# Gathered rows of experts 1 to 7 turned by VectorE instead of TensorE

## The chip, the cores and the metric

The kernel runs on one core of one Trainium2 chip. The time is device microseconds of one execution. Before the change it is 1012.99 us in the median of 3 runs (1011.71 to 1014.88).

## The reference

Three stages follow each other on 4 x 576 = 2304 tokens of 512 features, all in fp32. First an attention of 8 heads that goes through 32 packed keys a head. Then a noisy top-2 routing to 8 experts, of which each computes `relu(x @ w1[e]) @ w2[e]` (512 to 1024 to 512) on its tokens. Then one dense layer of 512 to 2048 to 512 with a sigmoid gate.

```python
p_packed = sm_attn(p, k, v)                 # softmax attention, 32 rows a head
x = sm_attn(q, p_packed, p_packed)          # to (2304, 512): row = token, columns = head, then dimension
noisy_logits = x @ w_gate + np.log1p(np.exp(x @ w_noise)) * noise
top2 = np.argpartition(-noisy_logits, 2, axis=1)[:, :2]     # softmax weights over the two
for e in range(8):
    for k in range(2):
        mask = top2[:, k] == e
        out[mask] += top2_w[mask, k, None] * (np.maximum(x[mask] @ w1[e], 0.0) @ w2[e])
h = out @ w_in
return (h / (1.0 + np.exp(-h))) @ w_out
```

## The kernel before

Every fp32 operand of a large product is kept as a high and a low part, and a product is three matmuls (high by high, high by low, low by high).

The attention stage makes the rows of `x` in tiles of 128 tokens: two matmuls a tile (L419) give 256 features each, ScalarE copies them into the tile `xr` (L424), and SyncE stores it to `xs` in DRAM (L426). Beside it run the routing (`route`) and the load of expert 0's weights: `load` (L124) fetches a piece of 512 KB into one of three buffers `raw` by one DMA on SyncE, and `split` (L109) makes the high part on ScalarE (L111) and the low part on VectorE, for expert 0 on GpSimd (L112). The routing ends with `idx` (L513), the token of every slot: 8 experts x 5 tiles x 128 slots.

The experts' stage goes through experts 0 to 7, each in a short block of two tiles (256 tokens) and a long block of three (384). A block has eight steps. A step makes 128 hidden features of the block (`first`, 12 matmuls, L167 to L169, into one of two PSUM buffers `hps`), ScalarE evicts them as `hh` (L190), VectorE subtracts for `hl` (L191), and two steps later `second` (L177 to L179) adds their part to the block's output.

The tokens of a block come from `xs`: `fetch` (L150) lets GpSimd issue one indirect DMA a tile (L155), which gathers 128 rows of 2 KB into one of five buffers `xg`. `transposed` (L141) then turns the tile, since the product wants features on partitions: four TensorE transposes of 128x128 into PSUM (L145), a copy to the high part `xha` or `xhb` on ScalarE (L147), and a subtraction to the low part `xla` or `xlb` on VectorE (L148). The hooks between the steps (`hook_a`, `hook_b`) place the turn of the other block's next tiles, the loads and splits of the next expert's weights, and the conversion of pieces of the last layer's weights (`load64`, L638 to L642, through two scratch buffers `t64`, stored to DRAM at L669). Expert 0's two tiles are gathered and turned ahead of its first block, its three others in the last steps of that block, and expert 1's first two behind it.

The order on each engine is set by a planner that places each instruction by a simulated timeline; in the experts' stage some are pinned to program order (`pin`), among them the splits and the TensorE transposes. Each engine works through its own order. SyncE issues all plain DMAs in one order, GpSimd the indirect ones.

Of the kernel before, what the change touches and what calls it, by code (L numbers as in the profile page):

```python
# [7 lines left out]
F32 = mybir.dt.float32  # L8
# [11 lines left out]
P = 128  # L20
# [3 lines left out]
ET = 5  # L24
# [20 lines left out]
def body(ctx: ExitStack, tc: tile.TileContext, q, k, v, p, wg, wn, noise, w1, w2, w_in, w_out, out):  # L45
# [32 lines left out]
    V.tensor_scalar(sbase, iota8, float(CAP), ident[:, 0:1], op0=OP.mult, op1=OP.mult)  # L78
    ilo = const.tile([P, P], F32)
    G.iota(ilo, pattern=[[1, P]], base=0, channel_multiplier=0, allow_small_or_imprecise_dtypes=True)  # L80
# [15 lines left out]
    idx = const.tile([P, E * ET], I32)  # L96
    idx0 = const.tile([P, TA], I32)
    few = const.tile([P, E], F32)

    M = {"pin": False, "w": 384, "hb": 3}  # L100

    def pin(ins):
        if M["pin"]:
            tc.keep_in_program_order(ins)
# [18 lines left out]

    def load(dst, src, c, eng=V):  # L124

        hi, lo = dst
        raw = raws.tile([P, 1024], F32, name="raw", tag="raw")
        nc.sync.dma_start(raw.rearrange("p (c f) -> p c f", c=c), src.rearrange("(c p) f -> p c f", p=P))
        later.append(lambda: split(hi, lo, raw, eng))

    def load_w1(dst, e, i, eng=V):
        load(dst[i], w1[e, :, i * 256:(i + 1) * 256], 4, eng)

# [7 lines left out]
    def transposed(src, xh, xl, j):  # L141

        ps = M["t"].tile([P, 4, P], F32, name="tps", tag="tr")
        for c in range(4):
            pin(T.transpose(ps[:, c, :], src[:, c * P:(c + 1) * P], ident))  # L145
        s = slice(j * P, (j + 1) * P)
        A.activation(xh[:, :, s], ps, AF.Copy)  # L147
        V.tensor_tensor(xl[:, :, s], ps, xh[:, :, s].bitcast(F32), op=OP.subtract)  # L148

    def fetch(src, ix, c0, n):  # L150
# [66 lines left out]
    with ExitStack() as ax:  # L217
# [150 lines left out]
        def unpacked(t, n, lg):  # L368
# [45 lines left out]
            for i in range(n):  # L414
                xr = sb.tile([P, 2, 256], F32, name="xr")
# [10 lines left out]
                nc.sync.dma_start(xs[r0:r0 + P, :], xr.rearrange("p a b -> p (a b)"))  # L426
            yield

        def route(t0, n, lg):
# [178 lines left out]
        for j, xg in enumerate(fetch(xs[0:EARLY * P, :], idx0, 0, TA)):  # L608
            transposed(xg, *X["a"], j)
        cnt = const.tile([P, E], F32)  # L610
        most = const.tile([P, 1], I32)
        rows = []
        for f in expert_block(0, 0, TA, X["a"]):
            run(r1, 2)
            if f == 4:
                for _ in r1:
                    pass
                rows = fetch(xs[:, :], idx, TA, TB) + fetch(xs[:, :], idx, ET, TA)
                c = pMx.tile([P, E], F32, name="c", tag="m")
                T.matmul(c, ones, seen_b, start=True, stop=True)  # L620
                V.tensor_tensor(cnt, c, few, op=OP.max)
                V.tensor_reduce(most, cnt, axis=AX.X, op=OP.max)
            if f > 4:
                transposed(rows[f - 5], *X["b"], f - 5)
        flush(0)
        for j in range(TA):
            transposed(rows[TB + j], *X["a"], j)

# [17 lines left out]
    def routed():  # L646
        ctx = mx = ExitStack()
        with mx:
# [29 lines left out]
            def combine(m):  # L678
# [4 lines left out]
                for j in range(n):  # L683
# [8 lines left out]
                    V.scalar_tensor_tensor(y[0], y[1], gates[:, t, 1:2], y[0], op0=OP.mult, op1=OP.add)  # L692
                    transposed(y[0], xh, xl, j)

# [42 lines left out]
            def hook_a(e, f):  # L737
                tick()
                if box["b"] and f:
                    transposed(box["b"].pop(0), *X["b"], TB - 1 - len(box["b"]))  # L740
                if f % 2:
# [6 lines left out]
                if f == 5 and e < E - 1:  # L748
                    box["a"] = fetch(xs[:, :], idx, (e + 1) * ET, TA)

            def hook_b(e, f):
# [17 lines left out]
                if f == 5:  # L769
                    box["b"] = fetch(xs[:, :], idx, (e + 1) * ET + TA, TB)  # L770

# [29 lines left out]
def general(tc, xs, ident, iota8, chosen, gates, w1, w2, w_in, w_out, out, load64):  # L801
# [3 lines left out]
    with tc.tile_pool(name="gc", bufs=1) as gc:  # L805
# [9 lines left out]
        with tc.For_i(0, NT, 1) as t, ExitStack() as fx:  # L815
# [21 lines left out]
            nc.sync.dma_start(x, xs[bass.ds(t * P, P), :])  # L837
            xT = turned(x, "xT")
            x2 = fs.tile([P, DM], F32, name="x2")
# [61 lines left out]
```

## Time and profile before

| | |
|---|---|
| median of 3 runs | 1012.99 us |
| the profiled execution's own time | 1011.33 us |
| its span, first to last instruction | 1009.4 us |
| TensorE busy | 974.0 us (96%) |
| VectorE busy | 436.5 us (43%) |
| ScalarE busy | 348.2 us (34%) |
| GpSimd busy | 208.4 us (21%) |
| mean granted TensorE clock | 0.981 |

The attention stage fills the time up to about 124 us, the experts' stage that up to about 600 us, the last layer the rest. PE is TensorE, DVE VectorE, ACT ScalarE, POOL GpSimd and SP SyncE; a q behind the name is the engine's queue of DMA issues and waits. A busy share is a mean over stages with different limits; the stage itself says what bounds it.

### The profile page before, as it was taken

The page shows a single profiled execution, that of the slowest core. Times are in us where ns is not written, and L with a number is a line of the kernel's source. Part 1 is how long each engine was busy: PE and PEld are TensorE (multiplying, and loading weights), DVE is VectorE, ACT ScalarE, POOL GpSimd, SP SyncE. Part 2 cuts the span into 40 slices and gives each one's busy share as a digit, 9 for nine tenths or more (in the row PEclk, how much of TensorE's full clock was granted, in tenths as well). Part 3 has the DMA queues.
Part 4 walks back from the last instruction along what each step waited for, and adds up shares of the span by engine and source line. Part 5 has one row for each costly group of instructions (what it writes and reads, how often), then busy time and mean ns, then how long its engine had stood idle before and what let it go on. Part 6 is the DMA issues. An engine that isn't in the chain of part 4 may idle for free.

```text
span 1009.4 us, 14342 instructions
## 1 busy us (share of the span) xinstructions
PE 974.0 (96%) x5672; PEld 836.8 (83%) x5672; DVE 436.5 (43%) x845; ACT 348.2 (34%) x631; POOL 208.4 (21%) x221
## 2 busy tenths in 40 slices
PE   6998899999999999999999998999999999999996
PEld 4775688999999989999999997888888888888885
DVE  4556763665657566565534457312212221111111
ACT  3575323433434343343423354322222222222221
POOL 2162011100101010010100117433323322222221
PEclk9988699999999999999999999999999999999999
DMA  9993223576757566574623346201111010001001
GB/s 254 254 281 121 90 74 115 188 219 185 229 151 235 176 201 214 186 230 149 227 84 115 125 160 185 74 21 32 32 42 42 21 48 6 1 0 42 1 1 44
DMA packets 80472, 122.47 MB, mean 121 GB/s; under 512 B 14608, under 2 KB 47376, under 8 KB 80400
## 3 DMA queue, kind: packets, MB, share of 16 engines
q1 hardware_dynamic: 74320, 101.57, 32.1%
q0 software_dynamic: 6080, 19.93, 6.6%
q8 instruction: 46, 0.75, 0.3%
q14 instruction: 26, 0.21, 0.1%
HBM read 93.17 MB, written 28.31 MB: 120 GB/s over the span
## 4 chain that ended last, share of the span: by engine, by line
PE 91%; DMA 3%; SPq 2%; DVE 1%; ACT 1%; POOL 1%; issue 1%; ACTq 0%; DVEq 0%; POOLq 0%
PE hps L167 14%; PE hps L168 14%; PE hps L169 14%; PE acc L177 14%; PE acc L178 14%; PE acc L179 13%; PE tps L145 2%; PE xp L419 2%; PE s L388 1%; DMA vm<-in_v_dram 1%; DMA km<-in_k_dram 1%; PE qp L381 1%; DMA y<-ys,slots 1%; SPq L236 0%; PE s L321 0%
## 5 line engine op out<-in xcount | busy, mean ns | idle before, releaser
L702 POOL TENSOR_TENSOR gl<-sg,gh 128x512 fp32r<-128x512 f32 (+1 forms) x80 | 96.0, 1201 | 253.9 <-ACT gh L701 238.6
L190 ACT ACTIVATE hh<-hps 128x384 fp32r<-128x384 f32 (+1 forms) x128 | 56.1, 438 | 253.7 <-PE hps L169 244.3
L698 DVE TENSOR_TENSOR sg<-hps,sg 128x512 f32<-128x512 f32 (+1 forms) x80 | 50.7, 635 | 195.8 <-ACT sg L697 195.4
L191 DVE SCALAR_TENSOR_TENSOR hl<-hps,hh 128x384 fp32r<-128x384 f32 (+1 forms) x128 | 62.8, 490 | 141.8 <-ACT hh L190 137.1
L155 POOL DMA_INDIRECT xg<-xs,idx x40 | 42.8, 1069 | 348.4 <-PE tps L145 296.7
L697 ACT ACTIVATE sg<-hps 128x512 f32<-128x512 f32 (+1 forms) x80 | 44.3, 553 | 187.9 <-PE hps L169 186.6
L701 ACT ACTIVATE gh<-sg 128x512 fp32r<-128x512 f32 (+1 forms) x80 | 47.1, 589 | 79.8 <-DVE sg L698 74.9
L688 POOL DMA_INDIRECT y<-ys,slots x36 | 37.5, 1043 | 117.1 <-DMA ys<-ysb 78.8
L148 DVE TENSOR_TENSOR xla<-tps,xha 128x512 fp32r<-128x512 f32 x26 | 18.0, 691 | 30.0 <-ACT xha L147 30.0
L419 PE MATMUL xp<-ppBD,a2T 128*128 128x272 f32 (+1 forms) x80 | 27.1, 481 | 2.1 <-ACT xr L51 1.7
L148 DVE TENSOR_TENSOR xlb<-tps,xhb 128x512 fp32r<-128x512 f32 x32 | 22.0, 687 | 15.1 <-ACT xhb L147 13.8
L691 DVE TENSOR_SCALAR y<-y,gates 128x512 f32<-128x512 f32 x18 | 10.3, 570 | 39.2 <-DMA y<-ys,slots 39.2
L692 DVE SCALAR_TENSOR_TENSOR y<-y,gates,y 128x512 f32<-128x512 f32 x18 | 14.7, 817 | 26.1 <-DMA y<-ys,slots 26.1
L147 ACT ACTIVATE xhb<-tps 128x512 fp32r<-128x512 f32 x32 | 19.1, 596 | 19.2 <-PE tps L145 18.7
L145 PEld LDWEIGHTS tps<-ident,xg 128*128 128x128 f32 x160 | 19.9, 141 | 5.3 <-issue 0.4
L145 PE MATMUL tps<-ident,xg 128*128 128x128 f32 x160 | 23.9, 272 | 0.2 <-issue 0.2
L641 DVE SCALAR_TENSOR_TENSOR t<-raw,t 128x512 int32<-128x512 int32 x32 | 22.2, 693 | 1.1
L642 DVE SCALAR_TENSOR_TENSOR t<-raw,t 128x512 int32<-128x512 int32 x32 | 22.1, 690 | 0.9
L147 ACT ACTIVATE xha<-tps 128x512 fp32r<-128x512 f32 x26 | 15.5, 597 | 19.7 <-PE tps L145 19.7
L638 ACT ACTIVATE t<-raw 128x512 f32<-128x512 f32 x32 | 21.1, 659 | 0.0
L388 PE MATMUL s<-ppT,qT 128*128 128x64 f32 x128 | 20.2, 315 | 0.0
L167 PE MATMUL hps<-xha,wa3h 128*128 128x256 f32 (+1 forms) x56 | 17.7, 316 | 2.2 <-DVE wb3l L112 1.5
(439 smaller groups left out, 2954.2 us busy)
## 6 DMA issues: line engine op xcount, KB each, us to landing
raw<-in_moe_w_dram SPq DMA_DIRECT2D x64, 512.0 KB
ys<-ysb SPq DMA_DIRECT2D x40, 256.0 KB
raw<-in_moe_w_in_dram SPq DMA_DIRECT2D x16, 512.0 KB
raw<-in_moe_w_out_dram SPq DMA_DIRECT2D x16, 512.0 KB
xs<-xr SPq DMA_DIRECT2D x18, 256.0 KB
km<-in_k_dram SPq DMA_DIRECT2D x8, 512.0 KB
vm<-in_v_dram SPq DMA_DIRECT2D x8, 512.0 KB
qm<-in_q_dram SPq DMA_DIRECT2D x8, 512.0 KB
```

The source lines that it names most:

```text
L145: pin(T.transpose(ps[:, c, :], src[:, c * P:(c + 1) * P], ident))
L167: T.matmul(ps, wh[:, c, s], xh[:, c, :n], start=c == 0, stop=False)
L168: T.matmul(ps, wh[:, c, s], xl[:, c, :n], start=False, stop=False)
L169: T.matmul(ps, wl[:, c, s], xh[:, c, :n], start=False, stop=c == 3)
L177: T.matmul(y, hh[:, s], wh[:, f % 2, :], start=f == 0, stop=False)
L178: T.matmul(y, hh[:, s], wl[:, f % 2, :], start=False, stop=False)
L179: T.matmul(y, hl[:, s], wh[:, f % 2, :], start=False, stop=f == last)
L190: A.activation(hh, ps, AF.Relu)
L191: V.scalar_tensor_tensor(hl, ps, 0.0, hh.bitcast(F32), op0=OP.max, op1=OP.subtract)
L419: T.matmul(xp[sl], aT[:, 2 * i + g, sl], ppBD[b, g], start=True, stop=True)
L698: V.tensor_tensor(sg, ps, sg, op=OP.mult)
L702: G.tensor_tensor(gl, sg, gh.bitcast(F32), op=OP.subtract)
```

## The change

The rows in `xs` are stored in another feature order. Feature number 128 b + 32 a + j (b and a from 0 to 3, j from 0 to 31) now stands in column 128 a + 32 b + j. ScalarE's copy into `xr` writes that order.

For experts 1 to 7 a tile is now fetched by four indirect DMAs instead of one. Each gathers a quarter of a row (512 bytes) for 128 partitions. In quarter g, the partitions 32 a to 32 a + 31 take quarter a of the rows of tokens 32 g to 32 g + 31. Their index `idx4` is made once behind `idx`: 16 small TensorE matmuls repeat the 32 indices in each group of partitions, and VectorE multiplies by 4 and adds a. VectorE then turns the whole 128x512 tile in blocks of 32x32 by one instruction into a scratch tile of the two `t64` buffers. ScalarE copies it to the high part and VectorE subtracts for the low part, both from SBUF.

Expert 0 keeps the gather of whole rows and the turn on TensorE. Its features then come out in the stored order, and so its `w1` pieces are loaded in that order, by four DMAs of 32 partitions instead of one. The path for overfull experts at the end of the program, which these inputs don't take, reorders the features it reads.

```diff
-    ilo = const.tile([P, P], F32)
+    ilo = dif
...
+    idx4 = const.tile([P, 4, E * ET], I32)
+    quad = const.tile([P, 1], F32)
+    for a in range(4):
+        V.memset(quad[32 * a:32 * a + 32], float(a))
...
-        nc.sync.dma_start(raw.rearrange("p (c f) -> p c f", c=c), src.rearrange("(c p) f -> p c f", p=P))
+        if runs:
+            for b in range(4):
+                nc.sync.dma_start(raw[32 * b:32 * b + 32].rearrange("j (a f) -> j a f", a=4),
+                                  src[b * P:(b + 1) * P].rearrange("(a j) f -> j a f", a=4))
+        else:
+            nc.sync.dma_start(raw.rearrange("p (c f) -> p c f", c=c), src.rearrange("(c p) f -> p c f", p=P))
...
-        load(dst[i], w1[e, :, i * 256:(i + 1) * 256], 4, eng)
+        load(dst[i], w1[e, :, i * 256:(i + 1) * 256], 4, eng, e == 0)
...
+    def runs(t):
+        return t.rearrange("p (a b j) -> p b a j", a=4, b=4)
+
+    def fetch4(c0, n):
+        tiles = []
+        for c in range(c0, c0 + n):
+            xg = M["s"].tile([P, DM], F32, name="xg", tag="xg", bufs=5)
+            for g in range(4):
+                G.indirect_dma_start(out=xg[:, g * P:(g + 1) * P], out_offset=None,
+                                     in_=xs[:, :].rearrange("n (a f) -> (n a) f", a=4),
+                                     in_offset=bass.IndirectOffsetOnAxis(ap=idx4[:, g, c:c + 1], axis=0))
+            tiles.append(xg)
+        return tiles
+
+    def turned4(src, xh, xl, j):
+        xt = M["s"].tile([P, 512], F32, name="xturn", tag="t64")
+        V.transpose(xt, src)
+        v = xt.rearrange("p (g b i) -> p b g i", g=4, b=4)
+        hi, lo = (x[:, :, j * P:(j + 1) * P].rearrange("p b (g i) -> p b g i", g=4) for x in (xh, xl))
+        pin(A.activation(hi, v, AF.Copy))
+        V.tensor_tensor(lo, v, hi.bitcast(F32), op=OP.subtract)
...
-                    cp(A, xr[:, g, :], xp[:, 0:256])
+                    cp(A, runs(xr)[:, 2 * g:2 * g + 2], xp[:, 0:256].rearrange("p (b a j) -> p b a j", b=2, a=4))
...
+                V.tensor_scalar(idx_f, idx_f, 0.0, float(N - 1), op0=OP.max, op1=OP.min)
+                i4 = pMx.tile([P, 4, E * ET], F32, name="i4", tag="m")
+                for g in range(4):
+                    for a in range(4):
+                        T.matmul(i4[32 * a:32 * a + 32, g, :], ident[:, 32 * g:32 * g + 32], idx_f, start=True, stop=True,
+                                 tile_position=(0, 32 * a))
+                V.tensor_scalar(idx4, i4, 4.0, quad[:, 0:1], op0=OP.mult, op1=OP.add)
...
-                rows = fetch(xs[:, :], idx, TA, TB) + fetch(xs[:, :], idx, ET, TA)
+                rows = fetch(xs[:, :], idx, TA, TB)
+                ahead = fetch4(ET, TA)
...
-            transposed(rows[TB + j], *X["a"], j)
+            turned4(ahead[j], *X["a"], j)
...
-                    transposed(box["b"].pop(0), *X["b"], TB - 1 - len(box["b"]))
+                    turned4(box["b"].pop(0), *X["b"], TB - 1 - len(box["b"]))
...
-                    box["a"] = fetch(xs[:, :], idx, (e + 1) * ET, TA)
+                    box["a"] = fetch4((e + 1) * ET, TA)
...
-                    transposed(box["a"].pop(0), *X["a"], TA - 1 - len(box["a"]))
+                    turned4(box["a"].pop(0), *X["a"], TA - 1 - len(box["a"]))
...
-                    box["b"] = fetch(xs[:, :], idx, (e + 1) * ET + TA, TB)
+                    box["b"] = fetch4((e + 1) * ET + TA, TB)
```

SyncE's order where expert 0's first weight pieces (`raw`) are loaded, among the last loads of q, k and v; first before, then after.

```order
L128 DMA raw<-in_moe_w_dram 128x4x256 x3
L247 DMA qm<-in_q_dram 128x4x256
L238 DMA vr<-in_v_dram 64x4x64
L238 DMA kr<-in_k_dram 64x4x64
L247 DMA qm<-in_q_dram 128x4x256
L238 DMA vr<-in_v_dram 64x4x64
L247 DMA qm<-in_q_dram 128x4x256 x2
L128 DMA raw<-in_moe_w_dram 128x4x256
```

```order
L134 DMA raw<-in_moe_w_dram 32x4x256 x5
L285 DMA qm<-in_q_dram 128x4x256
L276 DMA vr<-in_v_dram 64x4x64
L276 DMA kr<-in_k_dram 64x4x64
L285 DMA qm<-in_q_dram 128x4x256
L134 DMA raw<-in_moe_w_dram 32x4x256 x7
L276 DMA vr<-in_v_dram 64x4x64
L285 DMA qm<-in_q_dram 128x4x256 x2
L134 DMA raw<-in_moe_w_dram 32x4x256 x2
```

The first piece is four issues instead of one, and the rest of the second and the third stand behind four loads that they stood ahead of.

VectorE's order from the last steps of expert 0's short block (hl of 128x256) to the first of its long block (128x384), before and after.

```order
L191 SCALAR_TENSOR_TENSOR hl<-hps,hh 128x256 x2
L148 TENSOR_TENSOR xlb<-tps,xhb 128x4x128 x2
L191 SCALAR_TENSOR_TENSOR hl<-hps,hh 128x256
L148 TENSOR_TENSOR xlb<-tps,xhb 128x4x128
L148 TENSOR_TENSOR xla<-tps,xha 128x4x128
L53 COPY ysb<-acc 128x512
L148 TENSOR_TENSOR xla<-tps,xha 128x4x128
L191 SCALAR_TENSOR_TENSOR hl<-hps,hh 128x384 x4
```

```order
L157 TENSOR_TENSOR xlb<-tps,xhb 128x4x128 x2
L182 STREAM_TRANSPOSE xturn<-xg 128x512
L229 SCALAR_TENSOR_TENSOR hl<-hps,hh 128x256
L157 TENSOR_TENSOR xlb<-tps,xhb 128x4x128
L53 COPY ysb<-acc 128x512
L186 TENSOR_TENSOR xla<-xturn,xha 128x4x128
L182 STREAM_TRANSPOSE xturn<-xg 128x512
L186 TENSOR_TENSOR xla<-xturn,xha 128x4x128
L229 SCALAR_TENSOR_TENSOR hl<-hps,hh 128x384 x3
```

The turn of expert 1's first tile stands ahead of the short block's last subtraction, that of its second ahead of the long block's first.

GpSimd's order from the gather of expert 0's first two tiles to the first gather of the last layer, before and after.

```order
L155 DMA xg<-xs,idx_103 128x512 x2
L155 DMA xg<-xs,idx 128x512 x38
L688 DMA y_5897<-ys,slots 128x512
```

```order
L193 DMA xg<-xs,idx_102 128x512 x2
L193 DMA xg<-xs,idx 128x512 x3
L173 DMA xg<-xs,idx_103 128x128 x140
L734 DMA y_5933<-ys,slots 128x512
```

35 issues of whole tiles became 140 of quarters, in the same place.

## Rows read from the trace of the kernel before

**Rows 1.** First part of the page.

```profile
span 1009.4 us, 14342 instructions
...
PE 974.0 (96%) x5672; PEld 836.8 (83%) x5672; DVE 436.5 (43%) x845; ACT 348.2 (34%) x631; POOL 208.4 (21%) x221
```

**Rows 2.** Busy time in stretches: one expert, a short block, a long one.

```profile
core 0: us, PE busy (x) PEld busy (x) DVE busy (x) ACT busy (x) POOL busy (x), PEclk, DMA share, GB/s
308.00:366.20 58.20, 58.20 (x334) 52.79 (x333) 36.05 (x56) 22.11 (x37) 5.53 (x5) 1.00 0.63 201
...
300.90:324.90 24.00, 24.00 (x159) 21.78 (x158) 16.37 (x26) 10.17 (x18) 3.64 (x3) 1.00 0.65 212
324.90:359.20 34.30, 34.30 (x178) 31.11 (x177) 19.76 (x32) 11.94 (x20) 1.89 (x2) 1.00 0.60 189
```

**Rows 3.** Chain of waits: start us, us, what.

```profile
191.31 0.23 PE acc L179
191.54 0.44 PE tps L145 x4
...
547.30 0.44 PE tps L145 x4
...
1000.42 3.33 DMA out_dram<-osb
```

**Rows 4.** Who waited for the turned tiles: us, times.

```profile
  POOL xg L155: 296.7, 28
```

**Rows 5.** Timeline of VectorE: start us, us, engine line op, [idle before].

```profile
283.24 0.43 DVE L639 TENSOR_SCALAR t<-t 128x512 f32<-128x512 f32 x1
...
315.62 0.69 DVE L148 TENSOR_TENSOR xlb<-tps,xhb 128x512 fp32r<-128x512 f32 x1
```

**Rows 6.** Timeline of SyncE and ScalarE in a short block.

```profile
316.93 0.32 SPq L669 DMA_DIRECT2D wf_in<-t  x1
...
319.47 0.66 ACT L638 ACTIVATE t<-raw 128x512 f32<-128x512 f32 x1
```

**Rows 7.** Timeline of GpSimd: issues of gathers.

```profile
142.42 0.94 POOL L155 DMA_INDIRECT xg<-xs,idx  x1 [23.61 <-DVE idx L513]
...
147.42 0.95 POOL L155 DMA_INDIRECT xg<-xs,idx  x1 [0.30 <-issue]
...
195.50 1.35 POOL L155 DMA_INDIRECT xg<-xs,idx  x1 [2.31 <-PE tps L145]
```

**Rows 8.** Timeline of GpSimd and VectorE: a gather and its first reader.

```profile
669.15 0.96 POOL L688 DMA_INDIRECT y<-ys,slots  x1 [0.15 <-issue]
...
672.55 0.75 DVE L692 SCALAR_TENSOR_TENSOR y<-y,gates,y 128x512 f32<-128x512 f32 x1 [2.48 <-DMA y<-ys,slots]
```

**Rows 9.** Timeline of VectorE and TensorE, expert 0's two blocks.

```profile
150.85 0.42 DVE L191 SCALAR_TENSOR_TENSOR hl<-hps,hh 128x256 fp32r<-128x256 f32 x1 [1.35 <-ACT hh L190]
...
155.03 0.44 PE L167 MATMUL hps<-xhb,wa0h 128*128 128x384 f32 x1 [1.46 <-DVE xla L148]
...
159.31 0.39 PE L177 MATMUL acc<-wa4h,hh 128*128 128x512 f32 x1
```

**Rows 10.** Timeline of SyncE, ScalarE and TensorE at the first weight piece.

```profile
46.53 1.69 SPq L128 DMA_DIRECT2D raw<-in_moe_w_dram  x3
...
50.58 1.06 ACT L111 ACTIVATE wa0h<-raw 128x1024 fp32r<-128x1024 f32 x1 [2.79 <-DMA raw<-in_moe_w_dram]
...
52.17 0.66 PE L336 MATMUL ap<-ident,a 128*128 128x128 f32 x4 [2.42 <-ACT a1T L51]
```

**Rows 11.** Busy time in two stretches of 5 us.

```profile
55.00:60.00 5.00, 5.00 (x22) 4.15 (x21) 4.03 (x8) 2.28 (x4) 3.76 (x2) 0.52 1.12 292
...
155.00:160.00 5.00, 4.97 (x27) 4.86 (x28) 0.56 (x1) 0.98 (x2) 2.08 (x3) 1.00 0.38 127
```

**Rows 12.** DMA queues: packets, MB, share of 16 engines.

```profile
q1 hardware_dynamic: 74320, 101.57, 32.1%
q0 software_dynamic: 6080, 19.93, 6.6%
```

More of the change, by code (lines that the diff above doesn't have):

```diff
@@ L122, in tick, with load @@
                 fn()
-    def load(dst, src, c, eng=V):
+    def load(dst, src, c, eng=V, runs=False):
         hi, lo = dst
         raw = raws.tile([P, 1024], F32, name="raw", tag="raw")
-        nc.sync.dma_start(raw.rearrange("p (c f) -> p c f", c=c), src.rearrange("(c p) f -> p c f", p=P))
+        if runs:
[4 more added lines that the diff above has]
+            nc.sync.dma_start(raw.rearrange("p (c f) -> p c f", c=c), src.rearrange("(c p) f -> p c f", p=P))
         later.append(lambda: split(hi, lo, raw, eng))
     def load_w1(dst, e, i, eng=V):
-        load(dst[i], w1[e, :, i * 256:(i + 1) * 256], 4, eng)
+        load(dst[i], w1[e, :, i * 256:(i + 1) * 256], 4, eng, e == 0)
     def load_w2(dst, e, i, eng=V):
@@ L144, in transposed @@
         for c in range(4):
-            pin(T.transpose(ps[:, c, :], src[:, c * P:(c + 1) * P], ident))
+            pin(T.transpose(ps[:, c, :], src(c), ident))
         s = slice(j * P, (j + 1) * P)
@@ L148, in transposed, with plain @@
         V.tensor_tensor(xl[:, :, s], ps, xh[:, :, s].bitcast(F32), op=OP.subtract)
+    def plain(t):
+        return lambda c: t[:, c * P:(c + 1) * P]
+    def runs(t):
[17 more added lines that the diff above has]
+        V.tensor_tensor(lo, v, hi.bitcast(F32), op=OP.subtract)
     def fetch(src, ix, c0, n):
@@ L414, in unpacked @@
             for i in range(n):
-                xr = sb.tile([P, 2, 256], F32, name="xr")
+                xr = sb.tile([P, 512], F32, name="xr")
                 for g in range(2):
@@ L423, in unpacked @@
                         V.tensor_copy(lg[:, i, :], xp[:, 256:272])
-                    cp(A, xr[:, g, :], xp[:, 0:256])
+                    cp(A, runs(xr)[:, 2 * g:2 * g + 2], xp[:, 0:256].rearrange("p (b a j) -> p b a j", b=2, a=4))
                 r0 = (t + i) * P
-                nc.sync.dma_start(xs[r0:r0 + P, :], xr.rearrange("p a b -> p (a b)"))
+                nc.sync.dma_start(xs[r0:r0 + P, :], xr)
             yield
@@ L608, in body @@
         for j, xg in enumerate(fetch(xs[0:EARLY * P, :], idx0, 0, TA)):
-            transposed(xg, *X["a"], j)
+            transposed(plain(xg), *X["a"], j)
         cnt = const.tile([P, E], F32)
@@ L623, in body @@
             if f > 4:
-                transposed(rows[f - 5], *X["b"], f - 5)
+                transposed(plain(rows[f - 5]), *X["b"], f - 5)
         flush(0)
         for j in range(TA):
-            transposed(rows[TB + j], *X["a"], j)
+            turned4(ahead[j], *X["a"], j)
     def load64(raws, sbuf, src, last=None):
@@ L692, in combine @@
                     V.scalar_tensor_tensor(y[0], y[1], gates[:, t, 1:2], y[0], op0=OP.mult, op1=OP.add)
-                    transposed(y[0], xh, xl, j)
+                    transposed(plain(y[0]), xh, xl, j)
             def silu_split(ps, n):
@@ L837, in general @@
             nc.sync.dma_start(x, xs[bass.ds(t * P, P), :])
-            xT = turned(x, "xT")
+            xo = fs.tile([P, DM], F32, name="xo")
+            V.tensor_copy(xo.rearrange("p (b a j) -> p b a j", a=4, b=4), x.rearrange("p (a b j) -> p b a j", a=4, b=4))
+            xT = turned(xo, "xT")
             x2 = fs.tile([P, DM], F32, name="x2")
```

## The prediction

> **What bounds the kernel now.** I read the page's first part, then stretches of time one expert long, then the chain of waits, then who waited for the transposed tiles, and last the two places where TensorE does stand still. The reader is to see that TensorE holds 96% of a span of 1009.4 us [rows 1], and all of it in the experts' stage: the stretch from one expert's first turn to the next one's shows TensorE busy 58.20 of 58.20 us at clock 1.00, VectorE 36.05 [rows 2]. There the end moves by what TensorE issues and by nothing else. The chain has the turning of one gathered tile as a piece of 0.44 us [rows 3]: 33 such pieces lie from 191.5 to 547.3 us, two more (the rows of expert 1 that are turned ahead) behind expert 0's first block. It is the chain's piece that counts, not the busy time of the four matmuls, which overlap. The 58.20 us of an expert thus hold 5 x 0.44 = 2.2 us that the change takes off TensorE.
>
> **The steady stage, what goes.** 33 x 0.44 = **14.5 us**. The evictions of the old turn become two passes over SBUF and one is added: VectorE's block turn. No row shows one. The nearest rows are a one-source pass over 128x512 in SBUF, 0.43 us, and the subtraction that follows each turn today, 0.69 [rows 5]; below by a faster pass 0.4, above by a turn at a quarter of the subtraction's rate 2.8. I take 0.69, as the change's new subtraction reads the same 512 elements.
>
> The Trainium skill (VectorE: DVE Perf Modes, The three transpose paths) gives 311 ns for a 128x128 bf16 turn on VectorE; an estimate from it for four times the width is 1.24 us, inside these ends, and no run here shows it.
>
> Which block has room? The short block (two tiles, eight steps) has VectorE busy 16.37 of 24.00 us, the long one 19.76 of 34.30 [rows 2]. Afterwards the short block lasts 24.00 - 3 x 0.44 = 22.7 and holds 16.4 + 3 x 0.69 = 18.4 us of VectorE: 81%. A step is 22.7/8 = 2.84 us, of which the second product takes six matmuls of 0.23 [rows 3] = 1.38. With two PSUM buffers a group's buffer is asked for again 2.84 + 1.38 = 4.2 us after its last matmul; eviction and subtraction need about 1.0 of it, so VectorE or ScalarE may be 3.2 us late before TensorE notices.
>
> Two new waits come into that block. First, the turned rows share two scratch buffers with the converted weight pieces, and so the next piece's first pass on ScalarE waits for the store of the piece two steps back instead of four. Its store is issued at 316.93 in the row shown [rows 6] and ScalarE would start about 2.5 us later; a store takes 3.33 us at the end of the program [rows 3]. With VectorE's extra passes ScalarE then stands up to 2.4 us, and behind it stand the next eviction and its subtraction: below 3.2, so nothing. Without that cover it is 2.4 us in each of five experts. Second, the block turn waits for its four transfers. GpSimd already waits 296.7 us for the turns to release its buffers [rows 4]: it fetches nearly one expert ahead. Twenty issues of 1.25 us (start to start) [rows 7] are 25 us of some 56; at 1.35 + 0.30 us, the longest issue shown [rows 7], 33. Hidden either way.
>
> The Trainium skill (SBUF: State Buffer, SBUF: two separate sides) warns that a two-port VectorE pass locks GpSimd out while it writes descriptors. The 1.35 us beside the usual 0.95 may be that; by the rule the issues stretch, by the row to 33 us an expert, and the sum stays.
>
> **Behind expert 0's first block, what comes.** The index for the four-way fetch is made by 16 small matmuls and one pass (below 1 us), and GpSimd issues three whole tiles first, then eight quarters. The first issue is at 142.42 and the fifth at 147.42 [rows 7]. A gather lands 3.4 us after its issue begins (669.15 to 672.55) [rows 8]. So the fourth quarter of the first tile, the seventh issue, starts at 149.9 and lands at 153.3; that of the second, the eleventh, at 154.9 and 158.3. In the new order VectorE's turn of the first stands ahead of the subtraction of the block's last group, done from 150.85 today [rows 9], and the turn of the second ahead of the first subtraction of the next block; ScalarE's copy of it stands ahead of that block's first eviction. TensorE therefore waits about 2 us for the block's last two matmuls, and at the next block's second product: 158.3 + 0.7 turn + 0.6 copy + 0.5 eviction = 160.1 against 159.31 today [rows 9], +0.8, with the gain of those two tiles already in it. The index itself is later in the order by one small group of matmuls, up to 1.3 us: +2.1. I take **+1.5**; ends 0 (the waits already there at 155.03, 1.46 us, absorb it) and +4 (a TensorE that stood over 2 us comes back at half clock, as at 52 us, below).
>
> **The front, what comes.** Expert 0's first weights now come in 4 transfers a piece: 12 more issues on SyncE, 1.69/3 = 0.56 us each [rows 10]. Behind them on SyncE stand the last q and v loads. ScalarE waits 2.79 us for the first piece at 50.58, and TensorE behind it 2.42 us at 52.17 [rows 10]; the next stretch then runs at granted clock 0.52, about the lower level of 1.2 GHz [rows 11]. Three more issues ahead of the piece's last quarter: +1.7. The second and third piece follow in the new order behind other loads, complete near 53.6 and 55.9 us instead of about 48, and their splits stand on ScalarE ahead of evictions that TensorE needs: some +1.3 more. I take **+3**; ends -2 (the planner's new order elsewhere in this stage, which is not full) and +8 (each later split shows in full and the lower clock lasts longer).
>
> **The sum.** -14.5 + 1.5 + 3 = -10 us. The profiled execution took 1011.33 us (span 1009.4 and 1.9 around it), so about 1001.3 there. The median shown is 1012.99, 1.7 above it; from the median: **1003**. Ends of the terms together: -14.5 + 0 - 2 = 996.5 and, with +4 and +8, 1010.5.
>
> **Rivals.**
> *The front and the start cost nothing visible.* For it: the stage ahead of 125 us waits at many places, and a load that comes later may come in one of them. Against: the wait at 50.58 is on the chain now. Price: -14.5 and no more, 998.5.
> *The stalls bring the lower clock.* TensorE's wait of about 2 us behind expert 0 and a longer one at 52 us are each followed by half speed, as the row at 55 to 60 us shows: 2 to 4 us more at each. Both upper ends: 1010; no change to speak of. Against: the 1.46 us at 155.03 [rows 9] are followed by clock 1.00 [rows 11].
> *The quarters crowd the weight loads: slower.* Per MB the gather queue takes 6.6% for 19.93, the other 32.1% for 101.57 [rows 12]: 3.3 and 3.2 us of all sixteen engines a MB, though the packets differ by 2.4 times (3.3 and 1.4 KB). So a tile of 0.26 MB costs 0.88 us of DMA and, if bytes decide, the same in quarters. If instead each row costs what a 2 KB row costs, a tile costs 3.5. Three tiles are refetched in each short block, right as they are turned: +7.9 us in 22.7 that are 0.65 full [rows 2]. The weight pieces then arrive up to 7.9 us late, ScalarE and VectorE stand behind them, and of that 3.2 are covered: 4.7 us lost in each of six experts, 28 us: 1031. It decides from about 2.4 us a tile on: (2.4 - 0.88) x 3 = 4.6, less 3.2, times six is 8, and by 2.5 the gain is gone. Against it: the two queues' equal price a MB.
>
> The Trainium skill (DMA: Bandwidth & Descriptors, Measured) gives 0.95 us for a transfer of 64 KB and calls transfers under 64 KB bound by descriptors. By it a tile in quarters is an estimated 3.8 us, on this rival's side; no row shows a transfer of quarters yet.
>
> **How the numbers follow.** A kernel like this tells apart 0.3%, 3 us: faster is below 1009.95, slower above 1016.0. The forecast (1000 to 1008) has 0.60, the free front 0.15, the clock rival (1008 to 1014) 0.15, the crowded loads 0.10. Faster: 0.60 + 0.15 + half of the clock rival's 0.15 = 0.82; same: the other half and a tenth of the crowded loads' case that ends near before, 0.09; slower 0.09. The range from 997 to 1011 takes in the ends of the terms and leaves out the crowded loads and the top of the clock rival.
>
> **What would show it.** In the profile after: no turn in TensorE's rows from 160 to 598 us, an expert's stretch of 56.0 us with TensorE still full; block turns near 0.69 us; the wait of a split for its piece no longer than today. At the start: the second product of expert 0's long block near 160 plus what the front lost; ScalarE's first split near 52.3. An expert of 58 us or more, or a TensorE with gaps in it, would make the forecast wrong; so would a front longer by over 8 us.

## The result and the profile after

The changed kernel takes 1005.05 us in the median of 4 runs (1003.54 to 1005.92), the kernel before 1013.51 beside it (4 runs, 1011.71 to 1014.88). The ratio is 0.9916, with a 95% interval from 0.9896 to 0.9936: some 8.5 us faster. The forecast was 1003 (1000 to 1008), in a range from 997 to 1011. The profiled execution took 1005.28.

The first part of the page after, which answers to [rows 1]:

```profile
span 1003.5 us, 14316 instructions
...
PE 962.6 (96%) x5564; PEld 825.8 (82%) x5564; DVE 456.7 (46%) x886; ACT 347.6 (35%) x631; POOL 319.9 (32%) x326
```

TensorE lost 11.4 us of busy time, the span 5.9. VectorE gained 20 us and GpSimd 111. In the experts' stage TensorE is as full as before; the stretch of [rows 2], one expert long there:

```profile
core 0: us, PE busy (x) PEld busy (x) DVE busy (x) ACT busy (x) POOL busy (x), PEclk, DMA share, GB/s
308.00:366.20 58.20, 58.20 (x329) 52.91 (x328) 40.56 (x63) 22.34 (x38) 21.25 (x20) 1.00 0.67 207
```

The block turn in the view by tile (ns min/median/max, first and last start in us, then who waited for the tile it writes):

```profile
L182 DVE STREAM_TRANSPOSE xturn<-xg x35: 701/706/715, 156.7 to 537.8; 128x512 f32<-128x512 f32 x35
...
  POOL xg L173: 158.6, 27
```

It takes 0.71 us where 0.69 was taken. GpSimd still waits for it [rows 4], so it still fetches ahead. The DMA queues, beside [rows 12]:

```profile
q1 hardware_dynamic: 74512, 101.57, 32.4%
q0 software_dynamic: 7760, 19.93, 7.0%
```

The gather queue took 6.6% of 1009.4 us and takes 7.0% of 1003.5: 3.6 us of all sixteen engines more for 35 tiles, 0.1 us a tile. By these shares a tile in quarters costs the DMA engines about what a tile of whole rows costs.

Where the time went is read at four places that every kernel of this study has: expert 0's first product, the first gather that needs the whole index, the start of the last matmul of expert 0's long block, and the last layer's first sigmoid. The rows after (TensorE, GpSimd, TensorE, ScalarE):

```profile
126.84 0.72 PE L205 MATMUL hps<-xha,wa0h 128*128 128x256 f32 x1
...
146.61 0.95 POOL L193 DMA_INDIRECT xg<-xs,idx  x1 [25.76 <-DVE idx_f L552]
...
200.29 0.39 PE L217 MATMUL acc<-wa7h,hl 128*128 128x512 f32 x1
...
589.04 0.38 ACT L743 ACTIVATE sg<-hps 128x256 f32<-128x256 f32 x1 [2.14 <-PE hps L207]
```

and before (the gather is in [rows 7]):

```profile
123.86 0.39 PE L167 MATMUL hps<-xha,wa0h 128*128 128x256 f32 x1
...
191.15 0.39 PE L179 MATMUL acc<-wa7h,hl 128*128 128x512 f32 x1
...
594.79 0.38 ACT L697 ACTIVATE sg<-hps 128x256 f32<-128x256 f32 x1 [2.14 <-PE hps L169]
```

The front is 3.0 us longer. From there to the long block's end it was 67.29 us and is 73.45: +6.2, of which 1.2 lie ahead of the gather. From there to the sigmoid it was 403.64 and is 388.75: -14.9. The rest differs by 0.15.

The 6.2 us are read in TensorE's rows at the second product of expert 0's long block, and in the stretches around it:

```profile
157.75 0.74 PE L217 MATMUL acc<-wa7h,hl 128*128 128x512 f32 x2 [1.09 <-DVE hl L229]
...
162.46 0.34 PE L207 MATMUL hps<-xhb,wa0l 128*128 128x384 f32 x1
165.48 0.79 PE L215 MATMUL acc<-wa4h,hh 128*128 128x512 f32 x1 [2.68 <-ACT hh L228]
166.07 0.63 PE L216 MATMUL acc<-wa4l,hh 128*128 128x512 f32 x1
...
168.20 0.52 PE L205 MATMUL hps<-xhb,wa1h 128*128 128x384 f32 x1
...
171.90 0.85 PE L217 MATMUL acc<-wa4h,hl 128*128 128x512 f32 x3
```

```profile
160.00:165.00 5.00, 2.80 (x17) 2.48 (x15) 1.40 (x2) 0.69 (x2) 0.40 (x1) 0.99 0.35 121
165.00:170.00 5.00, 4.52 (x12) 3.94 (x13) 1.02 (x2) 0.81 (x2) 3.47 (x4) 0.50 0.15 39
170.00:175.00 5.00, 5.00 (x25) 4.79 (x24) 1.18 (x2) 0.49 (x1) 3.78 (x5) 0.83 0.18 52
```

TensorE stands for 2.68 us, and then works at granted clock 0.50, the level of 1.2 GHz, until about 172: six matmuls take 2.72 us from start to start and twelve 3.70, where they take 6 x 0.23 and 12 x 0.173 at clock 1.00. That is 3.0 us more. The last two matmuls of the short block waited 1.09 us, and the sixteen matmuls for the new index take 0.42. Gone are the 1.46 us of wait that stood here before [rows 9] and two turns of 0.44. With the 1.2 us ahead of the gather: 2.68 + 3.0 + 1.09 + 0.42 - 1.46 - 0.88 + 1.2 = 6.05 of the 6.2. The chain of waits names what TensorE stood for longest (pieces of 0.05 us and less left out):

```profile
159.13 3.50 DMA xg<-xs,idx
162.75 0.72 DVE xturn L182
163.50 0.64 ACT xha L185
164.16 0.70 DVE xla L186
164.94 0.50 ACT hh L228
165.48 0.79 PE acc L215
```

The eighth quarter of expert 1's first two tiles is issued at 159.13 and lands at 162.6; then come the turn, the copy and the subtraction, and only then the first eviction of the long block.

### The profile page after: what moved, and what is told of

It is laid out like the page before. It is cut to its first block, busy times and chain, and to the rows that moved or that the text cites. A ratio compares the mean times of both kernels' runs of the same rounds, so it can differ in the third digit from the quotient of the medians.

```text
span 1003.5 us, 14316 instructions
## 1 busy us (share of the span) xinstructions
PE 962.6 (96%) x5564; PEld 825.8 (82%) x5564; DVE 456.7 (46%) x886; ACT 347.6 (35%) x631; POOL 319.9 (32%) x326
## 4 chain that ended last, share of the span: by engine, by line
PE 86%; DVE 4%; DMA 4%; SPq 2%; POOL 2%; issue 1%; ACT 1%; POOLq 0%; DVEq 0%; ACTq 0%
PE hps L205 13%; PE hps L207 13%; PE hps L206 13%; PE acc L215 13%; PE acc L216 13%; PE acc L217 13%; PE xp L457 2%; PE s L426 1%; DMA vm<-in_v_dram 1%; PE tps L154 1%; DMA xg<-xs,idx 1%; POOL xg L173 1%; DMA km<-in_k_dram 1%; DVE rt_oa L531 1%; DMA y<-ys,slots 1%
## 5 line engine op out<-in xcount | busy, mean ns | idle before, releaser
L173 POOL DMA_INDIRECT xg<-xs,idx x140 | 149.5, 1068 | 193.0 <-DVE xturn L182 134.6
L182 DVE STREAM_TRANSPOSE xturn<-xg 128x512 f32<-128x512 f32 x35 | 24.8, 708 | 11.5 <-DMA xg<-xs,idx 5.9
L738 DVE SCALAR_TENSOR_TENSOR y<-y,gates,y 128x512 f32<-128x512 f32 x18 | 14.9, 826 | 25.9 <-DMA y<-ys,slots 25.9
L457 PEld LDWEIGHTS xp<-ppBD,a2T 128*128 128x128 f32 (+1 forms) x80 | 13.6, 215 | 8.1 <-ACT xr L51 4.2
L426 PEld LDWEIGHTS s<-ppT,qT 128*128 128x128 f32 x128 | 19.0, 227 | 0.6
L51 ACT ACTIVATE xr<-xp 128x256 f32<-128x256 f32 x36 | 13.3, 383 | 16.9 <-DVE lg L459 7.7
L193 POOL DMA_INDIRECT xg<-xs,idx x5 | 4.9, 986 | 44.5 <-DVE idx_f L552 25.8
L215 PE MATMUL acc<-wa4h,hh 128*128 128x512 f32 x40 | 16.5, 421 | 2.7 <-ACT hh L228 2.7
```

The lines of the kernel that those rows point to most:

```text
L173: G.indirect_dma_start(out=xg[:, g * P:(g + 1) * P], out_offset=None, in_=xs[:, :].rearrange("n (a f) -> (n a) f", a=4), in_offset=bass.In ...
L215: T.matmul(y, hh[:, s], wh[:, f % 2, :], start=f == 0, stop=False)
```

## The experiments

One table holds what the profiles show; times in us. Medians are of all runs of a kernel, the last three columns of its one profiled execution; for the reordering copy (1016.79) and the two turns (1020.80) that execution was several us quicker than the median. "Gather" is the first gather with the whole index, "start" from it to the last matmul of expert 0's long block, "steady" from there to the first sigmoid. Ratios are to the kernel before, beside it on the same chip.

| kernel | median | ratio, 95% interval | gather | start | steady |
|---|---|---|---|---|---|
| before | 1013.51 | | 142.42 | 48.73 | 403.64 |
| after | 1005.05 | 0.9916 (0.9896 to 0.9936) | 146.61 | 53.68 | 388.75 |
| one load a piece | 997.91 | 0.9869 (0.9824 to 0.9914) | 141.92 | 52.19 | 388.74 |
| whole rows | 1004.88 | 0.9922 (0.9891 to 0.9952) | 149.11 | 50.23 | 388.75 |
| both turns | 1022.48 | 1.0113 (1.0077 to 1.0150) | 147.75 | 53.73 | 403.41 |
| turn later | 1002.71 | 0.9898 (0.9860 to 0.9935) | 148.89 | 46.93 | 388.74 |
| reordering copy | 1027.21 | 1.0142 (1.0120 to 1.0165) | 148.69 | 62.90 | 388.75 |
| both repairs | 1026.33 | 1.0132 (1.0109 to 1.0156) | 144.54 | 75.86 | 388.74 |
| two turns | 1026.16 | none: 1015.96 to 1031.81 | 152.04 | 63.25 | 388.75 |
| four turns | 1030.43 | 1.0185 (1.0142 to 1.0228) | 147.41 | 76.63 | 388.70 |
| after, again | 1006.36 | 0.9942 (0.9926 to 0.9959) | 148.25 | 52.20 | 388.75 |
| both repairs, again | 997.23 | 0.9840 (0.9817 to 0.9863) | 146.62 | 47.70 | 388.75 |
| loads split with ScalarE | 1007.62 | 0.9946 (0.9923 to 0.9969) | 148.15 | 54.00 | 388.74 |
| loads split with GpSimd | 1010.19 | 0.9980 (0.9963 to 0.9997) | 158.13 | 46.71 | 388.74 |

The steady stage repeats to 0.05 us, whatever stands ahead of it. The gather scatters: by 1.6 and 2.1 us between the two profiles of the two kernels that ran on two chips. A front read from one profile has that uncertainty.

**One load a piece.**

```diff
-        load(dst[i], w1[e, :, i * 256:(i + 1) * 256], 4, eng, e == 0)
+        load(dst[i], w1[e, :, i * 256:(i + 1) * 256], 4, eng)
```

> Expert 0's four w1 pieces come by one DMA each again, in the plain order of features; left out is the arrangement of these weights in the stored order, so expert 0's products mix features. Everything else is as in the kernel after. Theory (the twelve more DMA issues on SyncE cost the front 2.7 us): the first product of expert 0's short block, at 126.84 us after and 123.86 before, comes back to within 0.7 us of 123.9, its first second product from 130.3 to about 127.6, and the whole is 2.5 to 3 us faster than after (about 1002.4). Rival (the front is longer because the planner orders the attention stage otherwise, or because of ScalarE's rearranging copy): that landmark stays at 126 or later and the time is within 1 us of after.

Expert 0's first product came at 123.38, the gather at 141.92, and the time is 7 us below after's, 4.8 by the ratios: more than expected, though the two intervals overlap. On the same chip the three kernels with four loads a piece have the gather at 147.75 to 149.11. By these profiles the four-part load, with the order that the planner makes of it, costs the front 5 to 7 us at this place. Later profiles show less: with one load and a reordering copy (below) the gather came at 144.54 to 148.69. The stall stayed (2.81 us).

**Whole rows.**

```diff
-            for g in range(4):
-                G.indirect_dma_start(out=xg[:, g * P:(g + 1) * P], out_offset=None,
-                                     in_=xs[:, :].rearrange("n (a f) -> (n a) f", a=4),
-                                     in_offset=bass.IndirectOffsetOnAxis(ap=idx4[:, g, c:c + 1], axis=0))
+            G.indirect_dma_start(out=xg[:, :], out_offset=None, in_=xs[:, :],
+                                 in_offset=bass.IndirectOffsetOnAxis(ap=idx[:, c:c + 1], axis=0))
```

> The tiles of experts 1 to 7 are fetched as whole rows by one indirect DMA each, as before, and still turned by VectorE in 32x32 blocks; left out is the arrangement that makes the turned blocks the tokens' columns. GpSimd issues 38 gathers instead of 143. Theory (quarters cost nothing in the steady stage; their serial issue of about 1.1 us each costs the start of expert 0's long block a stall of 2.9 us and 3 us of half clock): the stretches of 200 to 600 us keep TensorE full and last as long as after to within 1 us; the second product of the long block, at 165.5 us after, comes at 159.5 to 161 with a wait under 1 us, the clock stays 1.00 there, and the whole is 4 to 6 us faster than after (about 1000). Rival (quarters crowd the weight loads): the steady stage itself gets shorter by more than 2 us and the DMA queue's share falls well under 7.0%. Rival (the stall comes from VectorE's order, not from the issues): the stall stays above 2 us and the time is within 1.5 us of after.

The steady stage is the same to 0.01 us, so quarters crowd nothing there: that rival is gone. The start is 3.5 us shorter, not the 5 to 6 that the theory gave to the issues, and the whole is no faster. The tiles are there in time, but in this order VectorE makes both turns and both subtractions ahead of expert 0's last `xlb`, and TensorE stands for that:

```profile
161.65 0.44 PE L203 MATMUL hps<-xhb,wa0h 128*128 128x384 f32 x1 [1.67 <-DVE xlb L157]
```

The lower clock follows this shorter wait too: 160 to 165 us have a granted clock of 0.71.

So the issues are half of the matter. The other half is that turns for the next expert stand in VectorE's order ahead of work for this one.

**Both turns.**

```diff
         V.transpose(xt, src)
+        ps = M["t"].tile([P, 4, P], F32, name="tps", tag="tr")
+        for c in range(4):
+            pin(T.transpose(ps[:, c, :], src[:, c * P:(c + 1) * P], ident))
```

> The kernel after with the four TensorE transposes a tile kept beside the block turn, into a PSUM tile that nobody reads: 35 x 4 transposes back on TensorE and nothing else. Theory (in the steady stage the time is what TensorE issues, 0.44 us a tile): 33 x 0.44 = 14.5 us come back between 200 and 600 us, with the tiles of the start 14.5 to 15.4 us in all: about 1019.5 to 1020.5, and VectorE's extra passes cost nothing beside. Rival (part of the gain came from the evictions that left PSUM, or from a shorter wait on buffers): less than 12 us come back. Rival (the added VectorE passes cost TensorE something that the gain hides): then the both-turns kernel shows gaps in TensorE between 200 and 600 us, more than 2 us in all, or more than 16 us come back.

The steady stage is 14.66 us longer than after's and within 0.23 of before's. VectorE's passes, the new gather and the extra wait for stores are all still in it, and cost nothing; TensorE's four transposes are the whole gain of that stage. The total, 1022.48, is 2 us above the 1019.5 to 1020.5 that was expected.

**Turn later.**

```diff
-                ahead = fetch4(ET, TA)
...
-        for j in range(TA):
-            turned4(ahead[j], *X["a"], j)
...
-                if box["a"] and f:
+                if box["a"] and f > (3 if e == 0 else 0):
...
-            box["a"] = []
+            box["a"] = fetch4(ET, TA)
```

> The kernel after, but the first two tiles of expert 1 are fetched in the experts' stage and turned behind steps 4 and 5 of expert 0's long block instead of ahead of it; nothing is left out. Theory (ahead of the long block VectorE's turns wait for the last quarters, and behind them stand the subtractions that TensorE's second product needs: 2.9 us of wait, then 3 us of half clock): the second product of the long block comes at about 160 to 162.5 instead of 165.5, the granted clock from 155 to 175 us stays at 1.00, the block ends 5 to 6 us earlier than at 200.3, and the whole is 5 to 6 us faster (about 999.5). Rival (the queue of quarters only moves the wait: the turns come later in the block and hold up its subtractions then, or the next expert's short block waits for its tiles): under 2 us faster or slower, with TensorE's gap found later, between 165 and 205 us.

The second product came without a wait, and the stretch that stood at clock 0.50 is full at 1.00:

```profile
163.71 0.39 PE L215 MATMUL acc<-wa4h,hh 128*128 128x512 f32 x1
...
165.00:170.00 5.00, 5.00 (x28) 4.65 (x27) 0.59 (x2) 0.49 (x1) 3.78 (x5) 1.00 0.20 52
```

The start fell by 6.75 us, to 1.8 below before's, as two turns are gone from it too. The total fell by only 2.3 against after, and the two intervals overlap; the profiled front is 2.3 us later at the gather, though TensorE's order is the same up to there, and the four runs lie between 998.3 and 1004.4. The mechanism is shown in the stretch; its size in the total is not shown by this run.

**Reordering copy, both repairs, two turns, four turns.** The first keeps one load a piece in the plain order and lets VectorE copy expert 0's gathered tiles into that order; the second (shown) adds the later turn to it; the other two do the block turn twice and (shown) four times.

```diff
+    def restored(t):
+        xo = M["s"].tile([P, DM], F32, name="xo", tag="xg", bufs=5)
+        V.tensor_copy(xo.rearrange("p (b a j) -> p b a j", a=4, b=4), runs(t))
+        return plain(xo)
...
-            transposed(plain(xg), *X["a"], j)
+            transposed(restored(xg), *X["a"], j)
```

```diff
-        V.transpose(xt, src)
+        for _ in range(4):
+            V.transpose(xt, src)
```

> Expert 0's w1 pieces by one DMA each in the plain order, and instead VectorE copies each of expert 0's five gathered tiles into the plain feature order (0.4 to 0.7 us a tile) before TensorE turns it; nothing is left out. Theory (the four-part loads make the front longer: the index's first gather came at 141.9 with one load, at 146.6 to 149.1 with four, in five profiles): the first gather comes at 142 to 143.5, the stall ahead of expert 0's long block stays as in the kernel after (first gather to the block's last matmul 52.5 to 54.5 us), and the whole is 3 to 6 us faster than after's 1005 (999 to 1002). Rival (the reordering copies wait in VectorE's order and cost as much as the loads): within 1.5 us of after.

> Both repairs: expert 0's rows reordered by VectorE with one load a w1 piece, and expert 1's first two tiles fetched and turned inside expert 0's long block; nothing is left out. Theory (two separate terms: 4 to 6 us at the front, and 6.8 us between the first gather and the end of the long block, as the run with the later turn showed): first gather at 142 to 143.5, from there to the block's last matmul 47 to 48 us against 54.1 after, and the whole at 993 to 996. Rival (the two share one cause, the late index, so that the second repair brings nothing once the first is there): the stretch is 47 us either way but the time stays at 998 or above. Rival (the copies ahead of the turns delay the first block): first gather to the block's end over 49 us.

> The kernel after with the block turn done twice into the same tile: 35 more passes of 0.71 us on VectorE, nothing else. Theory (in the steady stage VectorE has room: a short block holds 18.4 us of work in 22.7, and may be 3.2 us late before TensorE notices): the time from the end of expert 0's long block to the last layer's first sigmoid, 388.4 us after, grows by less than 2 us, and TensorE stays full between 210 and 590 us; in all +0 to +3 us with about 1.4 of it at the start, where VectorE's turns are waited for. Rival (VectorE is near its bound in the short blocks): the stage grows by 0.71 a tile, up to 23 us.

> The kernel after with the block turn done four times into the same tile: 105 more passes of 0.71 us on VectorE, 2.1 us a tile. Theory (room of about 3.2 us behind each step and 4.3 us in a short block): a short block would hold 18.4 + 6.4 = 24.8 us of VectorE's work in 22.7, so TensorE must wait now, by 2 us or less in each of six short blocks where the long block ahead takes part of the work, at most 12 us in the stage between 388.4 us after and 400. Rival (VectorE's turns run early enough in the idle time of the long blocks): under 2 us more in the stage. Rival (each pass counts in full, 33 x 2.1 us): 70 us more.

All four, on one chip, were 13 to 17 us slower than before, and in the profiled executions it is all in the start: 63 to 77 us. There TensorE stands with nothing to wait for that the profile shows ("issue"). In both repairs and the four turns, which were profiled at their usual time, matmuls start 0.70 us apart or a multiple of it for many us; the other two show a few such gaps. SyncE needs 40 us to issue four weight loads, where the same kernel on another chip issued five in 18. Both repairs there:

```profile
202.30 0.48 PE L211 MATMUL hps<-xlb,wa3h 128*128 128x384 f32 x1 [1.62 <-issue]
203.70 0.48 PE L212 MATMUL hps<-xhb,wa3l 128*128 128x384 f32 x1 [0.92 <-issue]
204.40 0.48 PE L210 MATMUL hps<-xhb,wa3h 128*128 128x384 f32 x1 [0.22 <-issue]
205.10 0.48 PE L211 MATMUL hps<-xlb,wa3h 128*128 128x384 f32 x1 [0.22 <-issue]
```

```profile
171.27 40.01 SPq L137 DMA_DIRECT2D raw<-in_moe_w_dram  x4
```

The kernel before took its usual 1013.37 on that chip. So these four totals say nothing on the repairs. The gathers of the two kernels with one load, 148.69 and 144.54, lie ahead of the late stretch, and there the expected 142 to 143.5 did not come. The steady stage behind is undisturbed, and there the last two are clear: with 35 or 105 more block turns it stays at 388.75 and 388.70. With the fourfold turn VectorE is busy 41 of 50 us and TensorE all 50:

```profile
350.00:400.00 50.00, 50.00 (x276) 45.41 (x275) 41.05 (x68) 19.37 (x32) 18.03 (x17) 1.00 0.66 211
```

The theory expected up to 12 us for the fourfold turn, as a short block has no room for it; the rival, that the turns run earlier in the idle time of the long blocks, gave the size.

**After and both repairs, again, side by side on another chip.**

> The kernel after once more, unchanged, beside the kernel with both repairs. In the four runs before this one (both repairs, the reordering copy alone, the doubled and the fourfold turn), which shared a chip, every instruction in expert 0's long block came late: TensorE's matmuls 0.70 us apart with nothing to wait for, ScalarE 18 us without an instruction, SyncE's four weight loads 40 us in the issue, all while GpSimd issued quarters back to back. Theory A (it is the chip or its neighbours that day, not the kernels): beside each other on one chip the two stand in the order that the terms give, after at 1003 to 1007 and both repairs 10 us faster; or, where the chip does it again, after has it too and takes 1015 or more. Theory B (it is the kernels: where the turns of expert 1 or the copies come later, quarters and weight loads collide): after stays at 1003 to 1007 and both repairs take 1025 again.

> The kernel with both repairs once more, beside after on one chip. Theory A (the chip or its neighbours made the instructions late): 993 to 997, some 10 us faster than after in the same call, with the first gather at 142 to 144.6, and 47 to 48 us from it to the end of expert 0's long block; or both slow. Theory B (these kernels' own order brings it): 1025 again, with the long block of expert 0 at 60 us and matmuls 0.70 us apart in it, while after stays at 1005.

Neither shows late instructions. After takes 1006.36, 5.3 us below before there. Its stall is 2.68 us to the digit, but the lower clock ends sooner: after the six matmuls in 2.72 us the twelve take 2.28, so 1.5 us are lost where it was 3.0. That accounts for the difference between 53.68 and 52.20 in the table.

```profile
170.00:175.00 5.00, 5.00 (x28) 4.79 (x28) 1.27 (x2) 0.49 (x1) 3.78 (x5) 0.98 0.20 52
```

Both repairs take 997.23, 9.1 us less. There it beats both kernels of this case. Its start is 47.70 against 52.20: the later turn's part. Its gather is 1.6 us earlier, less than the one load alone gave. The lateness thus came on that chip at that time, in kernels that fetch in quarters and not in the kernel before; what it is stays open.

**Loads split between two issuers** (the kernel with the later turn).

```diff
-                nc.sync.dma_start(raw[32 * b:32 * b + 32].rearrange("j (a f) -> j a f", a=4),
+                (nc.sync if b % 2 else nc.scalar).dma_start(raw[32 * b:32 * b + 32].rearrange("j (a f) -> j a f", a=4),
```

> The kernel with the later turn, and of expert 0's four-part w1 loads two parts a piece issued by ScalarE instead of SyncE; nothing is left out. In ScalarE's order the first six stand in the first three places of the program, so that half of three pieces comes during the first 15 us. Theory (the front is longer because eight and more issues on SyncE push the second piece's parts behind other loads, and ScalarE, which splits in order, stands for them, 3.8 us at 60 us): the second piece's split, at 60 to 62 us with four loads on SyncE and 52 with one, comes at 53 to 56, the first gather of the index at 143 to 146 instead of 147 to 149, and the whole at 996 to 1000, 3 to 5 us below the later turn alone (1002.7). Rival (the transfers themselves, not their issues, are the cost; the early halves take the bandwidth of the first k and v loads): the front stays as long, first gather at 147 or later, and the time within 1.5 us of 1002.7 or above it.

> The same, with the two parts a piece issued by GpSimd, where six stand behind its first fills of buffers, before its first copies; nothing is left out. Theory (SyncE's issues are the cost): as with ScalarE, second piece's split at 53 to 56 us, first gather at 143 to 146, the whole at 996 to 1000; GpSimd has nothing to do there, so it may be 1 us better than ScalarE's, which has copies to make. Rival (the transfers are the cost): the front stays as long and the time is within 1.5 us of 1002.7 or above it.

Both fell to the rival. With ScalarE the second piece's split does come at 55.90, as expected, and still the gather is at 148.15; at the start TensorE waits 5.49 us for k, which now comes behind the early halves (0.98 and 2.51 us in the two profiles of after):

```profile
23.52 1.97 PE L348 MATMUL kp<-ident,km 128*128 128x128 f32 x8 [5.49 <-DMA km<-in_k_dram]
```

With GpSimd the gather is at 158.13, 9 us behind the later turn's 148.89. With ScalarE the long block stands 2.97 us again, although the turn is late: the short block's output is evicted later in this order, and the long block's first eviction waits for its store (2.50 us). So the later turn alone does not keep that eviction free; what counts is what the planner puts ahead of that eviction.

## Why the prediction was right, and where not

The forecast was -10 us. The medians moved by -8.5, the profiled pair by -5.9, and the repeat on another chip by -5.3. The large term held; one of the two small ones was missed by 4.7 us in the profiled pair. That the median lies only 2 us from 1003 is in part luck.

**Steady stage, -14.5: right in mechanism and size.** -14.9 us over 33 tiles, 0.45 each. Shown by the kernel with both turns, which gives back 14.66, and by twelve profiles at 388.70 to 388.75. The step on what hides VectorE's pass was right but far too cautious: 81% of a short block and 3.2 us of slack would have been used up by four turns, which cost nothing. The wait for the stores was put on ScalarE, up to 2.4 us a time, a figure that the rows shown do not give (3.33 - 2.54 is 0.8). In the trace ScalarE stands ahead of no piece's first pass. VectorE stands for stores ahead of seven block turns, 5.3 us in all, and TensorE stayed full:

```profile
L182 DVE STREAM_TRANSPOSE xturn<-xg x35: 701/706/715, 156.7 to 537.8; 128x512 f32<-128x512 f32 x35
...
  DMA wf_out<-t: 2.8, 3
  DMA wf_in<-t: 2.5, 4
```

The turn took 0.71 where 0.69 was taken. The estimate of 1.24 us from the Trainium skill (VectorE: DVE Perf Modes, The three transpose paths) was too high: the four 128x128 squares of one instruction do not each cost a turn of the 311 ns that the page gives for one in bf16.

**The crowded loads: refuted.** Taking the quarters away changed the steady stage by no more than 0.01 us. The queue's rows give (70.2 - 66.6)/35 = 0.1 us a tile more than the 0.88 before. The estimate of 3.8 us a tile from the Trainium skill (DMA: Bandwidth & Descriptors, Measured) does not hold for these indirect transfers; the measurement decides.

**The front, +3: right at its own mark, small by the next.** Expert 0's first product came 3.0 us later, in the second profile 4.4. But from there to the gather it is another 1.2 and 1.4 us longer in these two, and with one load a piece it is not (18.54 us, before 18.56). The mechanism that was named, later splits on ScalarE, is in the trace of ScalarE, where the second piece was split at 52.08 before:

```profile
60.06 1.06 ACT L115 ACTIVATE wa1h<-raw 128x1024 fp32r<-128x1024 f32 x1 [3.81 <-DMA raw<-in_moe_w_dram]
```

The first piece's split came at 51.78, near the 52.3 that was named, but after a wait of 3.81 us, longer than the 2.79 before. Yet getting the second split in time (55.90, with ScalarE issuing halves) did not shorten the front. Which of the loads' order, the transfers and the planner's other order costs what is not settled.

**Behind expert 0's first block, +1.5: the step that failed.** It measured +6.2, in the second profile +4.9; the upper end was +4. (Both count from expert 0's first product.) The issue times were right: the last quarter was to be issued at 154.9 with the gather at 142.42, and came at 159.13 with the gather at 146.61; the landing took 3.5 us where 3.4 was taken. The index came 1.2 us later, near the 1.3 that was allowed, but not for the sixteen matmuls that were named: they stand behind the first gather, at 148.08, and the kernel with one load has them too and is not later. What in the planner's order does it was not taken apart. Two things were mis-sized. The eviction stood not behind the copy alone, as the step had it, but behind the subtraction too, 0.8 us more, because the first `hh` of the new stage waits for the turned tile's subtraction (the chain above). The kernel opens a new scratch pool there, and presumably this tile takes over the memory that the subtraction still reads. And the clock: the step took the half clock into its upper end and the rivals, on the ground that 1.46 us of wait before had been followed by clock 1.00 [rows 9, 11]; a wait of 2.68 us was followed by 3.0 us lost at clock 0.50 in one execution and 1.5 in the other, and the kernel with whole rows has the lower clock behind 1.67 us. The "over 2 us" of the step's upper end does not fit that last row. The later turn takes wait and clock away together.

Sum in the profiled pair: 3.0 + 6.2 - 14.9 - 0.2 = -5.9, the span's difference. Of the rivals, the lower clock came true behind expert 0 and took 3.0 us of the gain, 1.5 in the repeat. At 52 us it lasted longer in the first profile (60 to 65 us at 0.75, before 1.00), but the mean granted clock up to the first gather is 0.88 in both. The free front and the crowded loads did not come true.

## What to carry to other kernels

Work taken off an engine that is full in a stage came back here to within half a us of 14.5, so such a term can be taken from the chain's rows. The cost of the same change sits where a stage starts and its inputs are not yet fetched: there a transfer cut in four lands only when its fourth issue has, and what is turned ahead for the next expert stands in front of what this one needs. Look there for the first eviction, and where TensorE will wait, put the lower clock into the term (1.5 and 3.0 us behind 2.68 us here) instead of leaving it to a rival.

## What was not expected of the hardware

The block turn of 128x512 fp32 takes 0.70 to 0.71 us, hardly more than a subtraction of that size (0.68), and three more of them a tile were invisible behind TensorE. An indirect transfer of 128 quarters of 512 bytes costs GpSimd the same 1.25 us from start to start as one of 128 whole rows, in a row of issues (median busy time 0.947 us for both, longest 1.98 and 1.35). On one chip, four kernels that fetch in quarters had instructions late for up to 30 us while GpSimd issued them back to back (matmuls 0.70 us apart, one SyncE issue of four loads 40 us); on three other chips the same pattern, and on one of them one of the very kernels, ran without it.
